# Longer loads and stores, and a release behind the last product, in a bf16 scale-and-add stream

## The chip, the cores and the metric

The kernel runs on one core of a Trainium2 chip. The metric is device time in microseconds (us), as a median of several executions; before and changed kernel were run on the same chip in the same rounds. A trace's *span*, from the first to the last instruction, is about 1.3 us shorter than the time of the execution that was traced. A ratio is the mean time of one kernel's runs over the mean of the other's of the same rounds, so it is not quite the ratio of the medians that are quoted beside it. Two kernels count as different when the ratio is clear of 2%.

## The reference

```python
B, S, D = 1024, 16, 512
x, y: (B, S, D) bf16;  gamma: (D,) bf16
def reference(x, y, gamma):
    return x + gamma * y
```

Flattened, x, y and the result are 16384 x 512. Each of the 128 partitions holds 128 consecutive rows of 512 elements, which is 128 KB. In this text "64 KB" is 64 such rows, the part of one partition; the transfer as a whole has 128 times as much, 8 MB.

## The kernel before

Loads are issued by SyncE, stores by ScalarE, so loads and stores are on two DMA queues (q1 and q10 of the page). VectorE does all the arithmetic: a product in place of y, and then a sum in place of that.

```python
PIECES = [32, 32, 32, 32]
X_AT = [0, 32, 0, 32]           # where in x_sb a piece of x goes: two places, each used twice
X_AFTER = [-1, -1, 0, 1]        # the sum that has to be done before the place is used again
SP = [('x', 0), ('y', 0), ('x', 1), ('y', 1), ('y', 2), ('x', 2), ('y', 3), ('x', 3)]
ACT = [('g',), ('s', 0, 0, 2), ('s', 1, 1, 2), ('s', 2, 2, 2), ('s', 3, 3, 3)]
EARLY = [('x', 0), ('y', 0), ('g',)]       # issued ahead of the start barrier

def _take(sem, n, eng):
    return eng.wait_ge(sem, n).then_inc(sem, -n)
...
    for c in range(n):
        yt = y_sb[:, piece(c), :]
        _take(s_y[c], 16, nc.vector)
        nc.vector.tensor_tensor(
            out=yt, in0=yt, in1=gamma_sb[:, None, :].to_broadcast([P, PIECES[c], D]), op=MULT
        ).then_inc(s_dve, 1)
        _take(s_x[c], 16, nc.vector)
        _take(s_dve, 1, nc.vector)
        nc.vector.tensor_tensor(out=yt, in0=x_tile(c), in1=yt, op=ADD).then_inc(s_add, 1)
```

A store `('s', a, b, k)` writes pieces a to b and waits until sum k is done. The first three stores all wait for sum 2. That is more than their data need: it keeps stores out of the way until the loads are nearly through.

Of the kernel before, what the change touches and what calls it, by code (L numbers as in the profile page):

```python
# [3 lines left out]


PIECES = [32, 32, 32, 32]

X_AT = [0, 32, 0, 32]
X_AFTER = [-1, -1, 0, 1]


SP = [('x', 0), ('y', 0), ('x', 1), ('y', 1), ('y', 2), ('x', 2), ('y', 3), ('x', 3)]
ACT = [('g',), ('s', 0, 0, 2), ('s', 1, 1, 2), ('s', 2, 2, 2), ('s', 3, 3, 3)]

EARLY = [('x', 0), ('y', 0), ('g',)]
MULT, ADD = mybir.AluOpType.mult, mybir.AluOpType.add


def _take(sem, n, eng):


    return eng.wait_ge(sem, n).then_inc(sem, -n)  # L22


def kernel(
    tc: tile.TileContext,
    x: bass.AP,
    y: bass.AP,
    gamma: bass.AP,
    out: bass.AP,  # L30
):



    nc = tc.nc
    P = nc.NUM_PARTITIONS
    tc.close()
    tc.compile()  # L38

    xf = x.flatten_outer_dims()  # L40
    yf = y.flatten_outer_dims()
    of = out.flatten_outer_dims()
    N, D = xf.shape
    rows = N // P
    n = len(PIECES)
    assert sum(PIECES) == rows
    starts = [sum(PIECES[:c]) for c in range(n + 1)]
    dt = xf.dtype
    xv = xf.rearrange("(p n) d -> p n d", p=P)
    yv = yf.rearrange("(p n) d -> p n d", p=P)  # L50
    ov = of.rearrange("(p n) d -> p n d", p=P)

    gamma_row = nc.alloc_sbuf_tensor("gamma_row", [1, D], dt).ap()
    ones_row = nc.alloc_sbuf_tensor("ones_row", [1, P], dt).ap()
    gamma_sb = nc.alloc_sbuf_tensor("gamma_sb", [P, D], dt).ap()
    y_sb = nc.alloc_sbuf_tensor("y_sb", [P, rows, D], dt).ap()
    x_rows = max(a + r for a, r in zip(X_AT, PIECES))
    x_sb = nc.alloc_sbuf_tensor("x_sb", [P, x_rows, D], dt).ap()
    gamma_ps = nc.alloc_psum_tensor("gamma_ps", [P, D], mybir.dt.float32).ap()

    sem = nc.alloc_semaphore
    s_gamma, s_ones, s_ps, s_dve = sem("s_gamma"), sem("s_ones"), sem("s_ps"), sem("s_dve")
    s_x = [sem(f"s_x{c}") for c in range(n)]
    s_y = [sem(f"s_y{c}") for c in range(n)]
    s_add, s_end, s_out = sem("s_add"), sem("s_end"), sem("s_out")

    def piece(a, b=None):
        return slice(starts[a], starts[(a if b is None else b) + 1])

    def x_tile(c):  # L70
        return x_sb[:, X_AT[c] : X_AT[c] + PIECES[c], :]

    early, stores = [], 0

    def ring(eng, what, known=-1):

        nonlocal stores
        for w in what:
            kind, args = w[0], w[1:]
            need = X_AFTER[args[0]] if kind == "x" else args[2] if kind == "s" else -1  # L80
            if need > known:
                eng.wait_ge(s_add, need + 1)
                known = need
            if kind == "g":
                i = eng.dma_start(out=gamma_row, in_=gamma.unsqueeze(0)).then_inc(s_gamma, 16)
            elif kind == "x":
                c = args[0]
                i = eng.dma_start(out=x_tile(c), in_=xv[:, piece(c), :]).then_inc(s_x[c], 16)
            elif kind == "y":
                c = args[0]  # L90
                i = eng.dma_start(out=y_sb[:, piece(c), :], in_=yv[:, piece(c), :])
                i.then_inc(s_y[c], 16)
            else:
                r = piece(args[0], args[1])
                i = eng.dma_start(out=ov[:, r, :], in_=y_sb[:, r, :]).then_inc(s_out, 16)
                stores += 1
            if w in EARLY:
                early.append(i.ins)

    ring(nc.sync, SP)  # L100
    ring(nc.scalar, ACT)


    nc.vector.memset(ones_row, 1.0).then_inc(s_ones, 1)  # L104
    _take(s_ones, 1, nc.tensor)
    _take(s_gamma, 16, nc.tensor)
    nc.tensor.matmul(gamma_ps, ones_row, gamma_row, start=True, stop=True).then_inc(s_ps, 1)  # L107
    _take(s_ps, 1, nc.vector)
    nc.vector.tensor_copy(out=gamma_sb, in_=gamma_ps).then_inc(s_dve, 1)  # L109
    _take(s_dve, 1, nc.vector)  # L110

    for c in range(n):
        yt = y_sb[:, piece(c), :]
        _take(s_y[c], 16, nc.vector)
        nc.vector.tensor_tensor(  # L115
            out=yt, in0=yt, in1=gamma_sb[:, None, :].to_broadcast([P, PIECES[c], D]), op=MULT
        ).then_inc(s_dve, 1)
        _take(s_x[c], 16, nc.vector)
        _take(s_dve, 1, nc.vector)
        nc.vector.tensor_tensor(out=yt, in0=x_tile(c), in1=yt, op=ADD).then_inc(s_add, 1)  # L120


    nc.scalar.sem_inc(s_end, 1)
    _take(s_end, 1, nc.sync)
    _take(s_add, n, nc.sync)
    _take(s_out, 16 * stores, nc.sync)

    main = nc.main_func.blocks[0].instructions
    names = {i.name for i in early}
    for b in nc.main_func.blocks[1:]:  # L130
        for i in [i for i in b.instructions if i.name in names]:
            b.instructions.remove(i)
    for k, i in enumerate(early):
        main.insert(1 + k, i)


# [1 line left out]
_INS = ['x', 'y', 'gamma']  # L138
_OUTS = [((1024, 16, 512), 'bfloat16')]


# [23 lines left out]
```

## Time and profile before

| | before |
|---|---|
| median | 120.41 us (120.14 to 120.46) |
| span of the trace | 119.5 us |
| bytes moved | 50.33 MB, 421 GB/s over the span |
| DMA queues' share of sixteen engines | 66.4% loads, 32.5% stores |
| VectorE busy | 70.2 us, 59% |

How to read it: the DMA share says what bounds the kernel. The page's groups of instructions (operation, result from operands, shape, count, busy us, mean ns, then idle time before them) and its list of DMA issues say what the pieces are:

```profile
L115 DVE TENSOR_TENSOR y_sb<-y_sb,gamma_sb 128x16384 bf16<-128x16384 bf16 x4 | 34.8, 8688 | 18.4 <-DVEq L22 18.4
L120 DVE TENSOR_TENSOR y_sb<-x_sb,y_sb 128x16384 bf16<-128x16384 bf16 x4 | 34.8, 8692 | 0.6
...
x_sb<-in_x_dram SPq DMA_DIRECT2D x4, 4096.0 KB, 21.5
y_sb<-in_y_dram SPq DMA_DIRECT2D x4, 4096.0 KB, 35.4
out_dram<-y_sb ACTq DMA_DIRECT2D x4, 4096.0 KB, 23.8
```

Eight VectorE instructions of 8.69 us each; the only idle time of note, 18.4 us, ends with a wait of its own sequencer (DVEq) for y. Twelve transfers of 4 MB. The prediction below shows the DMA rows, the windows and the timeline.

### The profile page before, as it was taken

The numbers are of one execution on the slowest core, as the hardware profiler recorded it, in microseconds if no ns is written. First come the engines' busy times: TensorE is split into PE (matmuls) and PEld (weight loads), VectorE is DVE, ScalarE is ACT, GpSimd is POOL, SyncE is SP. The second block draws the span as 40 slices with busy tenths as digits, with TensorE's granted clock in tenths as the row PEclk, the third lists the DMA queues.
The fourth block names the chain that finished last, engine by engine and source line by source line (L and its number), as shares of the span: only waits on it lengthen the run. The fifth ranks groups of instructions, "written<-read, shape, count | busy, mean of one in ns | idle before, by whom it ended". The sixth has DMA issues, their size and how long they took to land. (4 is left out here: it accounts for less than half of the span.)

```text
span 119.5 us, 84 instructions
## 1 busy us (share of the span) xinstructions
PE 0.6 (0%) x1; PEld 0.1 (0%) x1; DVE 70.2 (59%) x10; POOL 0.2 (0%) x4
## 2 busy tenths in 40 slices
PE   0100000000000000000000000000000000000000
PEld 0000000000000000000000000000000000000000
DVE  0100000699999289999999999999999600000000
POOL 0000000000000000000000000000000000000000
DMA  7989898998998989898989999898989898989995
GB/s 208 494 373 504 351 526 351 384 493 351 384 493 351 526 351 526 351 515 362 493 384 471 406 428 450 384 493 351 526 351 526 351 526 351 515 362 471 406 471 230
DMA packets 1730, 50.33 MB, mean 421 GB/s; under 512 B 193, under 2 KB 194, under 8 KB 194
## 3 DMA queue, kind: packets, MB, share of 16 engines
q1 hardware_dynamic: 1152, 33.55, 66.4%
q10 hardware_dynamic: 578, 16.78, 32.5%
HBM read 33.56 MB, written 16.78 MB: 421 GB/s over the span
## 5 line engine op out<-in xcount | busy, mean ns | idle before, releaser
L115 DVE TENSOR_TENSOR y_sb<-y_sb,gamma_sb 128x16384 bf16<-128x16384 bf16 x4 | 34.8, 8688 | 18.4 <-DVEq L22 18.4
L120 DVE TENSOR_TENSOR y_sb<-x_sb,y_sb 128x16384 bf16<-128x16384 bf16 x4 | 34.8, 8692 | 0.6
L109 DVE CAST gamma_sb<-gamma_ps 128x512 bf16<-128x512 f32 x1 | 0.7, 692 | 3.4 <-DVEq L22 3.4
L104 DVE MEMSET ones_row<- 1x128 bf16 x1 | 0.2, 165 | 2.0 <-PEq L38 2.0
L107 PE MATMUL gamma_ps<-gamma_row,ones_row 1*128 1x512 bf16 x1 | 0.6, 580 | 4.8 <-PEq L22 4.8
L107 PEld LDWEIGHTS gamma_ps<-gamma_row,ones_row 1*128 1x128 bf16 x1 | 0.1, 100 | 4.8 <-issue 4.8
L149 POOL MEMSET const-bfloat16-1.0<- 128x1 bf16 x1 | 0.1, 101 | 0.0
L149 POOL MEMSET const-uint8-127<- 128x1 uint8 x1 | 0.1, 101 | 0.0
L149 POOL MEMSET const-float32-0.0<- 128x1 f32 x1 | 0.1, 98 | 0.2 <-issue 0.2
L149 POOL MEMSET const-float32-1.0<- 128x1 f32 x1 | 0.1, 98 | 0.0
## 6 DMA issues: line engine op xcount, KB each, us to landing
x_sb<-in_x_dram SPq DMA_DIRECT2D x4, 4096.0 KB, 21.5
y_sb<-in_y_dram SPq DMA_DIRECT2D x4, 4096.0 KB, 35.4
out_dram<-y_sb ACTq DMA_DIRECT2D x4, 4096.0 KB, 23.8
gamma_row<-in_gamma_dram ACTq DMA_DIRECT2D x1, 1.0 KB
```

What stands on the lines that cost most here:

```text
L104: nc.vector.memset(ones_row, 1.0).then_inc(s_ones, 1)
L107: nc.tensor.matmul(gamma_ps, ones_row, gamma_row, start=True, stop=True).then_inc(s_ps, 1)
L109: nc.vector.tensor_copy(out=gamma_sb, in_=gamma_ps).then_inc(s_dve, 1)
L115: nc.vector.tensor_tensor(out=yt, in0=yt, in1=gamma_sb[:, None, :].to_broadcast([P, PIECES[c], D]), op=MULT).then_inc(s_dve, 1)
L120: nc.vector.tensor_tensor(out=yt, in0=x_tile(c), in1=yt, op=ADD).then_inc(s_add, 1)
L149: nc = _bacc.Bacc("TRN2", target_bir_lowering=False, num_devices=1)
```

## The change

The intent is fewer and longer transfers. y and x are loaded in halves of 64 KB rows, both x halves in one place; the stores are of 64, 32 and 32 KB. Since the first store would now be allowed as early as the second sum, before the second x half is even moving, a new semaphore `s_go` is to hold the stores until the last product is over.

```diff
-X_AT = [0, 32, 0, 32]
-X_AFTER = [-1, -1, 0, 1]
 
+SP = [('y', 0, 64), ('x', 0, 64, 0), ('y', 64, 128), ('x', 64, 128, 0)]
+ACT = [('g',), ('s', 0, 64), ('s', 64, 96), ('s', 96, 128)]
...
+DVE = [('m', 0), ('m', 1), ('a', 0), ('a', 1), ('m', 2), ('m', 3), ('go',), ('a', 2), ('a', 3)]
...
+            if kind == "s" and not went and ("go",) in DVE:
+                _take(s_go, 1, eng)
+                went = True
             if need > known:
-                eng.wait_ge(s_add, need + 1)
+                eng.wait_ge(s_add, need)
                 known = need
...
+    for kind, *args in DVE:
+        if kind == "go":
+            nc.vector.sem_inc(s_go, 1)
+            continue
...
+        if kind == "m":
+            need(y_loads, c)
+            g = gamma_sb[:, None, :].to_broadcast([P, PIECES[c], D])
+            nc.vector.tensor_tensor(out=yt, in0=yt, in1=g, op=MULT).then_inc(s_dve, 1)
+            open_mults += 1
```

`('m', c)` is the product of piece c, `('a', c)` its sum. A store now waits, besides `s_go`, only for the sums of its own pieces.

More of the change, by code (lines that the diff above doesn't have):

```diff
@@ L6 @@
 PIECES = [32, 32, 32, 32]
-X_AT = [0, 32, 0, 32]
-X_AFTER = [-1, -1, 0, 1]
-SP = [('x', 0), ('y', 0), ('x', 1), ('y', 1), ('y', 2), ('x', 2), ('y', 3), ('x', 3)]
-ACT = [('g',), ('s', 0, 0, 2), ('s', 1, 1, 2), ('s', 2, 2, 2), ('s', 3, 3, 3)]
-EARLY = [('x', 0), ('y', 0), ('g',)]
+SP = [('y', 0, 64), ('x', 0, 64, 0), ('y', 64, 128), ('x', 64, 128, 0)]
+ACT = [('g',), ('s', 0, 64), ('s', 64, 96), ('s', 96, 128)]
+EARLY = (2, 1)
+DVE = [('m', 0), ('m', 1), ('a', 0), ('a', 1), ('m', 2), ('m', 3), ('go',), ('a', 2), ('a', 3)]
 MULT, ADD = mybir.AluOpType.mult, mybir.AluOpType.add
@@ L56 @@
     y_sb = nc.alloc_sbuf_tensor("y_sb", [P, rows, D], dt).ap()
-    x_rows = max(a + r for a, r in zip(X_AT, PIECES))
+    x_loads = [w for w in SP + ACT if w[0] == "x"]
+    y_loads = [w for w in SP + ACT if w[0] == "y"]
+    stores = [w for w in SP + ACT if w[0] == "s"]
+    for loads in (x_loads, y_loads, stores):
+        assert sum(w[2] - w[1] for w in loads) == rows
+    x_rows = max(w[3] + w[2] - w[1] for w in x_loads)
     x_sb = nc.alloc_sbuf_tensor("x_sb", [P, x_rows, D], dt).ap()
@@ L62, with meets, pieces_of, x_at @@
     s_gamma, s_ones, s_ps, s_dve = sem("s_gamma"), sem("s_ones"), sem("s_ps"), sem("s_dve")
-    s_x = [sem(f"s_x{c}") for c in range(n)]
-    s_y = [sem(f"s_y{c}") for c in range(n)]
-    s_add, s_end, s_out = sem("s_add"), sem("s_end"), sem("s_out")
-    def piece(a, b=None):
-        return slice(starts[a], starts[(a if b is None else b) + 1])
-    def x_tile(c):
-        return x_sb[:, X_AT[c] : X_AT[c] + PIECES[c], :]
-    early, stores = [], 0
-    def ring(eng, what, known=-1):
-        nonlocal stores
-        for w in what:
-            kind, args = w[0], w[1:]
-            need = X_AFTER[args[0]] if kind == "x" else args[2] if kind == "s" else -1
+    s_load = {w: sem("s_" + "_".join(map(str, w[:2]))) for w in x_loads + y_loads}
+    s_add, s_go, s_end, s_out = sem("s_add"), sem("s_go"), sem("s_end"), sem("s_out")
+    added = [a for kind, *a in DVE if kind == "a"]
+    order = {a[0]: k for k, a in enumerate(added)}
+    def meets(a, b, c, d):
+        return a < d and c < b
+    def pieces_of(a, b):
+        return [c for c in range(n) if meets(starts[c], starts[c + 1], a, b)]
+    def x_at(row):
+        return next(w[3] + row - w[1] for w in x_loads if w[1] <= row < w[2])
+    def frees(w):
+        old = x_loads[: x_loads.index(w)]
+        old = [v for v in old if meets(v[3], v[3] + v[2] - v[1], w[3], w[3] + w[2] - w[1])]
+        return [c for v in old for c in pieces_of(v[1], v[2])]
+    early = []
+    def ring(eng, what, n_early):
+        known, went = 0, False
+        for k, w in enumerate(what):
+            kind = w[0]
+            need = frees(w) if kind == "x" else pieces_of(w[1], w[2]) if kind == "s" else []
+            need = max((order[c] + 1 for c in need), default=0)
+            if kind == "s" and not went and ("go",) in DVE:
+                _take(s_go, 1, eng)
+                went = True
             if need > known:
-                eng.wait_ge(s_add, need + 1)
+                eng.wait_ge(s_add, need)
                 known = need
@@ L86, in ring @@
             elif kind == "x":
-                c = args[0]
-                i = eng.dma_start(out=x_tile(c), in_=xv[:, piece(c), :]).then_inc(s_x[c], 16)
+                to = x_sb[:, w[3] : w[3] + w[2] - w[1], :]
+                i = eng.dma_start(out=to, in_=xv[:, w[1] : w[2], :]).then_inc(s_load[w], 16)
             elif kind == "y":
-                c = args[0]
-                i = eng.dma_start(out=y_sb[:, piece(c), :], in_=yv[:, piece(c), :])
-                i.then_inc(s_y[c], 16)
+                r = slice(w[1], w[2])
+                i = eng.dma_start(out=y_sb[:, r, :], in_=yv[:, r, :]).then_inc(s_load[w], 16)
             else:
-                r = piece(args[0], args[1])
+                r = slice(w[1], w[2])
                 i = eng.dma_start(out=ov[:, r, :], in_=y_sb[:, r, :]).then_inc(s_out, 16)
-                stores += 1
-            if w in EARLY:
+            if k < n_early:
                 early.append(i.ins)
-    ring(nc.sync, SP)
-    ring(nc.scalar, ACT)
+    ring(nc.sync, SP, EARLY[0])
+    ring(nc.scalar, ACT, EARLY[1])
     nc.vector.memset(ones_row, 1.0).then_inc(s_ones, 1)
@@ L110, with need @@
     _take(s_dve, 1, nc.vector)
-    for c in range(n):
-        yt = y_sb[:, piece(c), :]
-        _take(s_y[c], 16, nc.vector)
-        nc.vector.tensor_tensor(
-            out=yt, in0=yt, in1=gamma_sb[:, None, :].to_broadcast([P, PIECES[c], D]), op=MULT
-        ).then_inc(s_dve, 1)
-        _take(s_x[c], 16, nc.vector)
-        _take(s_dve, 1, nc.vector)
-        nc.vector.tensor_tensor(out=yt, in0=x_tile(c), in1=yt, op=ADD).then_inc(s_add, 1)
+    landed, open_mults = set(), 0
+    def need(loads, c):
+        for w in loads:
+            if w not in landed and meets(starts[c], starts[c + 1], w[1], w[2]):
+                _take(s_load[w], 16, nc.vector)
+                landed.add(w)
+    for kind, *args in DVE:
+        if kind == "go":
+            nc.vector.sem_inc(s_go, 1)
+            continue
+        c = args[0]
+        yt = y_sb[:, starts[c] : starts[c + 1], :]
+        if kind == "m":
[3 more added lines that the diff above has]
+            open_mults += 1
+        else:
+            need(x_loads, c)
+            if open_mults:
+                _take(s_dve, open_mults, nc.vector)
+                open_mults = 0
+            at = x_at(starts[c])
+            xt = x_sb[:, at : at + PIECES[c], :]
+            nc.vector.tensor_tensor(out=yt, in0=xt, in1=yt, op=ADD).then_inc(s_add, 1)
     nc.scalar.sem_inc(s_end, 1)
@@ L125 @@
     _take(s_add, n, nc.sync)
-    _take(s_out, 16 * stores, nc.sync)
+    _take(s_out, 16 * len(stores), nc.sync)
     main = nc.main_func.blocks[0].instructions
```

## The prediction

Rival A's sum came to 120.6 us: the time before, 120.4, with 0.35 for the restart and 0.1 for the stores added, less a gain from longer transfers. Of that gain only the 0.03 us of five boundaries comes from the trace. B's 120.6 stands on the same parts.

> **What bounds the kernel now.** I read the page's DMA rows first, because the reference is a pure stream: x and y in, x + gamma * y out, 50.33 MB in all.
>
> ```profile
> DMA  7989898998998989898989999898989898989995
> DMA packets 1730, 50.33 MB, mean 421 GB/s; under 512 B 193, under 2 KB 194, under 8 KB 194
> q1 hardware_dynamic: 1152, 33.55, 66.4%
> q10 hardware_dynamic: 578, 16.78, 32.5%
> ```
>
> The row of tenths never falls below 7, and the two queues (q1 the loads, q10 the stores) together fill 98.9% of sixteen engines' span. Next, windows cut where that row seemed to change (columns: busy time of PE, PEld, DVE, POOL, then clock, DMA share, GB/s):
>
> ```profile
> 18.00:39.00 21.00, 0.00 (x0) 0.00 (x0) 16.79 (x2) 0.00 (x0) 1.00 0.98 406
> 39.00:80.00 41.00, 0.00 (x0) 0.00 (x0) 38.14 (x6) 0.00 (x0) 1.00 1.00 432
> 118.00:119.50 1.50, 0.00 (x0) 0.00 (x0) 0.00 (x0) 0.00 (x0) 1.00 0.01 0
> ```
>
> So the kernel is a start, a full pipe, and an end. The trace's packet records say it finer: every large packet is 32 KB, 1536 of them, 96 on each engine; the usual distance between starts on one engine is 1.2094 us; 96 x 1.2094 = 116.1. The rest of the 119.5 us span: first packet 1.0 after the issue, 0.65 longer than later ones, 0.8 lost between 18 and 39 us (packets up to 1.42 us there), 0.35 spread between first and last engine, 0.4 from the last packet to the last landing mark. A DMA boundary costs almost nothing: 1.215 instead of 1.209 us. The timed 120.41 is the span and about 0.9.
>
> VectorE is busy 70.2 us of 119.5 and is not the bound, but it decides when buffers come free and when stores go. The timeline shows that:
>
> ```profile
> 4.83 0.58 PE L107 MATMUL gamma_ps<-gamma_row,ones_row 1*128 1x512 bf16 x1 [4.83 <-PEq L22]
> 22.06 8.69 DVE L115 TENSOR_TENSOR y_sb<-y_sb,gamma_sb 128x16384 bf16<-128x16384 bf16 x1 [15.81 <-DVEq L22]
> ...
> 42.16 8.69 DVE L115 TENSOR_TENSOR y_sb<-y_sb,gamma_sb 128x16384 bf16<-128x16384 bf16 x1 [2.57 <-DVEq L22]
> 51.00 8.69 DVE L120 TENSOR_TENSOR y_sb<-x_sb,y_sb 128x16384 bf16<-128x16384 bf16 x1
> 59.61 8.69 DVE L115 TENSOR_TENSOR y_sb<-y_sb,gamma_sb 128x16384 bf16<-128x16384 bf16 x1
> 59.72 0.33 SPq L88 DMA_DIRECT2D x_sb<-in_x_dram  x1
> ...
> 77.17 17.78 ACTq L95 DMA_DIRECT2D out_dram<-y_sb  x4
> ```
>
> Three things to see. (1) The stores are issued at 77.17, when the last load still has about 3.2 us to run (its last packet ends at 80.42), so the pipe never empties. (2) The product at 59.61 starts before the sum ahead of it is over (51.00 + 8.69 = 59.69), though a wait of VectorE's sequencer stands between them: that sequencer works ahead of the datapath. The trace has it more directly: the wait for x's first piece, behind the product of 22.06, was taken at 22.10, not at 30.75. (3) gamma, on the other queue, had landed by 4.69 and its matmul ran at 4.83, with 16 packets per engine queued on q1 until 21.6: two queues share an engine in turn, they do not wait for each other to empty.
>
> [...]
>
> **The change part by part.** *Fewer, longer transfers.* Twelve DMAs of the large kind become seven, rows of 32 KB become 64 KB except in the last two stores. Five boundaries at 0.006 us are 0.03 us. If rows become packets, an engine has 56 instead of 96[...]. The bytes do not change[...].
>
> *Loads and VectorE.* Landings follow bytes. The first 8 MB land at 21.93 as now, the second (x) at 42.03. Products of pieces 0 and 1 run 22.06 to 39.4, hidden. Sums start at 42.16; two unbroken instructions take 8.61 + 8.69, so they end at 59.46. Only then may the second x half be issued, at about 59.5 (SyncE's issue now follows a sum by 0.03). The second y half drains at 60.7 to 61.06. From a dead start, issue to the effective begin of the stream was 1.0 + 0.65 to 0.85 us, so the stream restarts at about 61.2: a loss of about 0.35 us, instead of none now.
>
> *The release.* VectorE takes y's second half at 61.43 (the sixth 4 MB landed at 61.41), product 2 runs 61.54 to 70.2, product 3 to 78.84. The diff intends the stores to go then. But the release is a semaphore instruction of VectorE's sequencer with nothing to wait for, placed behind the pushed products. The order listing shows it is not attached to a product, and by point (2) the sequencer does not wait for the product's end. With both products pushed at once it fires at about 61.7; ScalarE's other condition, two sums, has been met since 59.5. Then an 8 MB store shares the engines with the 8 MB x load almost from its start. x leads by some 4 us, 61.2 to 65; its other 15.4 us take double, to 95.8, landing at 96.2 instead of 80.8. Sum 2 runs 96.3 to 105.0. Store 0 is through at about 61.2 + 38.7 = 99.9. The second store waits for sum 2: issued at 105.0, flowing at 106.75. So the pipe is dry for about 6.9 us. Sum 3 ends at 113.6, ahead of the second store's end, and the last 8 MB take 19.35: 106.75 + 19.35 + 0.4 = 126.5 span, 127.4 timed. Counting instead in packet turns (x ends at 95.1) gives 126.9. I take 127.0.
>
> **The rivals.** *A, the release works as meant.* It fires at 78.9, stores get their first packet at 79.9 or later against a pipe that drains at 80.4 to 80.8: loss 0 to 0.2. Sums 2 and 3 end at 90 and 98.6, each far ahead of its store's turn. [...] For it: the plain intent of the diff. Against it: the 22.10 mark.
> *B, the sequencer is held until the last product enters the datapath*, 70.15. Store 0 joins at about 73 and x has some 7.5 us left, which take 15: x lands at 88, sum 2 ends at 96.9, store 0 at about 99.9. The second store is issued 3 us ahead of its turn, so the pipe stays full: 120.6 again. For it: before shows only one instruction waiting behind a running one. [...]
> *C, as worked out above*: 127.0, from 125.5 to 129 by how soon the store's packets take turns.
> *D, longer packets or fewer marks are worth more than I find*, or the 0.8 us of slow packets goes away with y first: 119.5 at best. The fixed parts, 116.1 + 1.0 + 0.65 + 0.35 + 0.4 + 0.9 = 119.4, leave no room for 118.0.
>
> **Range and chances.** C gets about 0.62, A and B together 0.36, D's extreme 0.02. A and B lie within 2%. The result is two-peaked, 120 to 121.5 or 125.5 to 129; a range for eight in ten has to reach from 119.8 to 128.8, with 127.0 as the likelier peak.
>
> **What would show it right or wrong.** C is right if ACT's first store is issued at 61 to 63, VectorE idles from 78.8 to about 96 before sum 2, the DMA row has a hole of several us at about 100, and the second store's issue follows sum 2 at about 105. B: first store at about 70.2, no hole. A: first store at 78.9. In all cases the x load should be issued at about 59.5, with a dip of some tenths of a us at 61, and large packets should number 896 if rows are packets. I am wrong in the main if stores issued early do not share with the load (x still landing at 81 with a store issued at 62), or if the release waits for the datapath.

## The result

| | before | changed |
|---|---|---|
| median | 120.39 us (120.14 to 120.46, 6 runs) | 131.41 us (131.19 to 131.95, 6 runs) |
| ratio | | 1.0931, interval 1.0905 to 1.0958 |
| span of the trace | 119.5 us | 130.6 us |
| VectorE busy | 70.2 us | 70.0 us |
| last landing mark of the last x load | 80.84 us | 100.74 us |

It is slower by 11 us. The page of the changed kernel shows where they are (rows of 40 slices of 3.26 us each, busy tenths and GB/s):

```profile
DVE  0020002999993999994999980000000999992000
DMA  9997997997977977979969899989996003899987
GB/s 321 422 542 321 502 462 321 522 442 321 622 341 321 642 321 321 642 321 321 321 301 502 381 402 522 402 361 522 402 422 281 0 0 161 371 432 482 422 381 321
DMA packets 1010, 50.33 MB, mean 385 GB/s; under 512 B 113, under 2 KB 114, under 8 KB 114
q1 hardware_dynamic: 576, 33.55, 61.4%
q10 hardware_dynamic: 434, 16.78, 29.8%
```

The bytes are the same. The DMA row, full to the end before, has a hole of two slices of zero with a 6 and a 3 beside them, and the GB/s row has its two zeros in the same place. VectorE has a gap of some seven slices ahead of its last block of work. The timeline tells what hangs on what:

```profile
41.46 17.29 DVE L154 TENSOR_TENSOR y_sb<-x_sb,y_sb 128x16384 bf16<-128x16384 bf16 x2 [2.14 <-DVEq L21]
58.78 0.33 SPq L106 DMA_DIRECT2D x_sb<-in_x_dram  x1
60.69 17.29 DVE L145 TENSOR_TENSOR y_sb<-y_sb,gamma_sb 128x16384 bf16<-128x16384 bf16 x2 [1.94 <-DVEq L21]
60.88 57.77 ACTq L112 DMA_DIRECT2D out_dram<-y_sb  x3
100.99 17.29 DVE L154 TENSOR_TENSOR y_sb<-x_sb,y_sb 128x16384 bf16<-128x16384 bf16 x2 [23.01 <-DVEq L21]
```

The two products start at 60.69 and end at 77.98. The first store is issued at 60.88, which is 0.2 us after the first of them *started*, 8.4 us before the second one did and 17 us before the end that was meant. (The row of ACTq covers all three stores: the trace has the other two issues at 109.71 and 118.31, each 0.03 us after a sum.) The x load, issued at 58.78, lands only at 100.74, so that VectorE stands still for 23 us before its last two sums. The table of waits gives the same:

```profile
DVE y_sb L154 <- DVEq L21: 25.1, 2, 23.0
DVE y_sb L145 <- DVEq L21: 15.5, 2, 13.5
```

The windows (columns as in the prediction: length, busy times, clock, DMA share, GB/s) show the stages:

```profile
58.00:66.00 8.00, 0.00 (x0) 0.00 (x0) 6.06 (x2) 0.00 (x0) 1.00 0.86 262
66.00:98.00 32.00, 0.00 (x0) 0.00 (x0) 11.98 (x2) 0.00 (x0) 1.00 1.01 436
98.00:102.00 4.00, 0.00 (x0) 0.00 (x0) 1.01 (x1) 0.00 (x0) 1.00 0.42 180
102.00:110.00 8.00, 0.00 (x0) 0.00 (x0) 8.00 (x2) 0.00 (x0) 1.00 0.00 0
110.00:118.00 8.00, 0.00 (x0) 0.00 (x0) 8.00 (x1) 0.00 (x0) 1.00 1.06 455
```

The same cut of the kernel before:

```profile
58.00:66.00 8.00, 0.00 (x0) 0.00 (x0) 8.00 (x2) 0.00 (x0) 1.00 1.06 459
66.00:98.00 32.00, 0.00 (x0) 0.00 (x0) 28.28 (x4) 0.00 (x0) 1.00 0.99 426
102.00:110.00 8.00, 0.00 (x0) 0.00 (x0) 0.00 (x0) 0.00 (x0) 1.00 0.99 426
```

From 66 to 98 the load and the store share the engines and together move as much as ever (436 GB/s). So sharing does not waste the engines there. The loss is after it: nothing at all moves from 102.8 to 110.55, because the first 8 MB of the result are out and the next store waits for sum 2, which waited for x. A smaller loss lies between 58 and 66, where packets of 262 GB/s start, against 459 before; a packet counts where it starts, so the long ones make this look worse than it is.

### The profile page after: what moved, and what is told of

The parts are those of the page before. It is cut to its first block, busy times and chain, and to the rows that moved or that the text cites. A ratio compares the mean times of both kernels' runs of the same rounds, so it can differ in the third digit from the quotient of the medians.

```text
span 130.6 us, 75 instructions
## 1 busy us (share of the span) xinstructions
PE 0.6 (0%) x1; PEld 0.1 (0%) x1; DVE 70.0 (54%) x10; POOL 0.2 (0%) x4
```

## The experiments

My theory (1) after the result: the release runs ahead of the products, load and store then take turns on every engine, x lands 20 us late, and the chain "x, sum 2, second store" leaves the engines dry. Rivals: (2) the long loads into one place are slow by themselves, whatever the release does; (3) mixing loads and stores on the engines costs in itself. Twelve kernels were run; all gave the reference's result. Each is compared with the kernel before in its own rounds. The rounds were on three chips, where the kernel before had medians of 120.31 to 120.66 us, so a few tenths between two rows of the table mean nothing. go_first, no_go, before_early, no_go32 and no_go32b were executed twice, best3 and the changed kernel six times, the others four times. Of rel_end and rel_end32 the interval reaches to both sides of 2%.

Where the text below speaks of packet records, these are the trace's single DMA packets. They do not name their engine; I follow an engine from a packet's end to the packet that starts there. "The slowest engine" is the one whose x data end last.

| run | median us | ratio | interval |
|---|---|---|---|
| changed kernel | 131.41 | 1.0931 | 1.0905 to 1.0958 |
| rel_end | 122.98 | 1.0214 | 1.0175 to 1.0253 |
| rel_mid | 124.56 | 1.0343 | 1.0287 to 1.0398 |
| go_first | 131.20 | 1.0897 | 1.0855 to 1.0939 |
| no_go | 143.25 | 1.1884 | 1.1841 to 1.1926 |
| rows32 | 123.59 | 1.0259 | 1.0226 to 1.0291 |
| before_early | 121.70 | 1.0099 | 1.0048 to 1.0151 |
| before_s64 | 120.44 | 0.9987 | 0.9953 to 1.0021 |
| rel_end32 | 122.81 | 1.0202 | 1.0152 to 1.0252 |
| best1 | 120.90 | 1.0032 | 1.0007 to 1.0057 |
| best3 | 120.69 | 1.0026 | 1.0004 to 1.0048 |
| no_go32 | 125.37 | 1.0412 | 1.0376 to 1.0449 |
| no_go32b | 125.19 | 1.0378 | 1.0310 to 1.0447 |

### rel_end: a release that waits for both products

```diff
-            nc.vector.sem_inc(s_go, 1)
+            nc.vector.wait_ge(s_dve, open_mults).then_inc(s_go, 1)
```

> The release waits for both products' completion marks, so that it comes at their end (about 78 us) and not at 60.75. Theory 1 (the 10 us are the early release alone): the store is issued at 78.1, the x load has the engines to itself and lands at about 81.5, no hole at 103 to 110; 120.9 us, 120.2 to 121.6, with some 0.5 to 1.5 us lost where the x load restarts the pipe at 60. Theory 2 (the long x load in one place is slow by itself): x still lands well after 85 and the time stays over 125.

Measured: 122.98 us. The timeline:

```profile
58.70 0.33 SPq L106 DMA_DIRECT2D x_sb<-in_x_dram  x1
60.62 17.29 DVE L145 TENSOR_TENSOR y_sb<-y_sb,gamma_sb 128x16384 bf16<-128x16384 bf16 x2 [1.94 <-DVEq L21]
78.09 22.32 ACTq L112 DMA_DIRECT2D out_dram<-y_sb  x3
82.74 17.30 DVE L154 TENSOR_TENSOR y_sb<-x_sb,y_sb 128x16384 bf16<-128x16384 bf16 x2 [4.83 <-DVEq L21]
```

Its page has this row in place of the one with the hole:

```profile
DMA  9799779977997799779798799999999889999992
```

The first store now goes at 78.09 and x has landed at 82.5; VectorE's long gap is gone, and so is the hole. One line of the kernel is worth 131.41 - 122.98 = 8.4 of the 11 us. Theory 2 falls as the main cause, but not altogether: the expected 120.2 to 121.6 was missed by 1.4 us. The packet records of this run show two places on the slowest engine. At 60 us, where the x load could only be issued at 58.70 and y's last packet ended at 60.11, the next packet ends 1.4 us later than an unbroken stream would have it. Between 77 and 82 us, where stores follow loads, packets of 2.7 to 3.8 us instead of 2.42 add 1.3. Such terms are not exact to the tenth: rel_end32 below has the same two with 1.7 and 0.8.

### rel_mid and go_first: the place of the release

rel_mid waits for one product's mark:

```diff
-            nc.vector.sem_inc(s_go, 1)
+            nc.vector.wait_ge(s_dve, 1).then_inc(s_go, 1)
```

> The release comes at the end of the first of the two products, 69.4 us. Theory 1: the store shares with the rest of the x load only; x lands at 89 to 92, sum 2 ends at 98 to 101, about when store 0 leaves the pipe dry, so the time is 120.5 to 123.5 us, near the version released at the end. Theory 2: over 125. Were any overlap of a store with the load to cost in proportion to its length, about 126.

Measured: 124.56 us, above my band. The store goes at 69.65 and x lands at 93.1:

```profile
69.65 41.41 ACTq L112 DMA_DIRECT2D out_dram<-y_sb  x3
93.40 17.29 DVE L154 TENSOR_TENSOR y_sb<-x_sb,y_sb 128x16384 bf16<-128x16384 bf16 x2 [15.32 <-DVEq L21]
```

Sum 2 ends at 102.09, and by the packet records an engine then stands for 1.8 us on the mean. So the direction is theory 1's, and x was again later than I had worked out; the reason is under rows32.

go_first keeps the bare release but puts it ahead of both products:

```diff
+            if c == 2:                    # behind the wait for y, in front of product 2
+                nc.vector.sem_inc(s_go, 1)
```

> The changed kernel with the release moved in front of both products, right behind the wait for y's second half. If the release never waited for a product, its place among them does not matter: it fires some 0.1 us sooner and the time is that of the changed kernel, 131.4 us (130.8 to 132.2). If the place behind two products did hold it for part of their time, clearly slower, up to the 143 us of the run without a release.

```profile
60.65 17.29 DVE L146 TENSOR_TENSOR y_sb<-y_sb,gamma_sb 128x16384 bf16<-128x16384 bf16 x2 [2.04 <-DVEq L21]
60.68 57.58 ACTq L112 DMA_DIRECT2D out_dram<-y_sb  x3
100.59 17.29 DVE L155 TENSOR_TENSOR y_sb<-x_sb,y_sb 128x16384 bf16<-128x16384 bf16 x2 [22.65 <-DVEq L21]
```

Measured: 131.20 us, and the same timeline to 0.4 us. In front of the products or behind them, the release is the same: as written it never waited for a product. In the changed kernel's trace the release stands at 60.745, 0.06 us after product 2 began and 8.55 us before product 3 did. So the sequencer had gone past product 3 in the list before that product started, at 69.295.

### no_go: no release at all

```diff
-DVE = [..., ('m', 2), ('m', 3), ('go',), ('a', 2), ('a', 3)]
+DVE = [..., ('m', 2), ('m', 3), ('a', 2), ('a', 3)]
```

> The release is taken out; the first store waits for the two sums alone and goes at 58.8 us, with the x load. If the release as written holds nothing back but 2 us, this is as slow as the changed kernel or a little slower, 131 to 134 us. If it did hold the store for longer in some useful way, clearly more than 135.

```profile
58.73 0.33 SPq L106 DMA_DIRECT2D x_sb<-in_x_dram  x1
58.74 71.09 ACTq L112 DMA_DIRECT2D out_dram<-y_sb  x3
112.17 17.29 DVE L154 TENSOR_TENSOR y_sb<-x_sb,y_sb 128x16384 bf16<-128x16384 bf16 x2 [34.23 <-DVEq L21]
```

Measured: 143.25 us, a miss. The bare release holds the store for only 2 us, and these are worth 12. x lands at 111.9, 11.2 us later than in the changed kernel. Three things differ in the packet records. One x packet per engine goes ahead of the first store packet, where the changed kernel has two; so one store packet more, 2.4 us, lies before x's end. Between 66 and 98 us the packets are longer, 3.01 us for x and 2.68 for the store on the mean, where the changed kernel has 2.42 throughout; seven turns of both make 7 x (3.01 + 2.68 - 4.84) = 6.0 us. And from 66 to 104 us the packets fill only 96.5% of the engines' time (in the changed kernel, from 66 to 98, all of it), which makes some 1.3 us. The sum, 9.7, is about the 9.4 us by which x's data end later on the mean of the engines (105.7 against 96.3). The rest of the 11.2 is that the engines no longer keep together: x's data end between 103.1 and 109.2, in the changed kernel between 95.4 and 98.0. Why packets stretch here and not in the changed kernel I tried to learn with no_go32 and no_go32b, below.

### rows32: shorter store rows, the early release left in

```diff
-ACT = [('g',), ('s', 0, 64), ('s', 64, 96), ('s', 96, 128)]
+ACT = [('g',), ('s', 0, 32), ('s', 32, 64), ('s', 64, 96), ('s', 96, 128)]
```

> The early release stays; the first store of 64 KB rows becomes two of 32 KB rows. If engines take turns by packet, a 64 KB x packet alternates with a 32 KB store packet: x lands at about 90 instead of 100.7, sum 2 ends at about 99, before the first two stores leave the pipe dry at 100 to 103: 121 to 123.5 us. If they share by bytes, or if mixing loads with stores is what costs, nothing changes: 130 to 132 us.

```profile
60.99 49.39 ACTq L112 DMA_DIRECT2D out_dram<-y_sb  x4
92.72 17.29 DVE L154 TENSOR_TENSOR y_sb<-x_sb,y_sb 128x16384 bf16<-128x16384 bf16 x2 [14.63 <-DVEq L21]
```

Measured: 123.59 us, 7.8 less than the changed kernel by nothing but the length of the store's rows. The same bytes of load and store share the engines from the same moment, and x lands at 92.5 instead of 100.7. Sharing by bytes, or a price on mixing (theory 3), would have left it at 131. In the changed kernel's records all sixteen engines take turns by packet: after two packets of x alone, a store and an x packet follow each other six times, 2.42 us each. And here a packet is a row: there are 640 packets of 65536 bytes. A 64 KB x packet (2.42 us) that waits for a 64 KB store packet moves half the time; one that waits for 32 KB (1.21 us) moves two thirds of it.

This run also explains why x was later than I worked out in each case. Compare the last end of an x data packet with the last landing mark of that load (us from the span's start, packet records and landing marks):

| run | rows of the store beside it | last x data | last x mark | between |
|---|---|---|---|---|
| before | none yet | 80.42 | 80.84 | 0.4 |
| rel_end | just starting | 82.15 | 82.50 | 0.35 |
| rows32 | 32 KB | 90.89 | 92.47 | 1.6 |
| no_go32b | 32 KB | 92.30 | 93.88 | 1.6 |
| rel_mid | 64 KB | 90.37 | 93.15 | 2.8 |
| changed | 64 KB | 97.96 | 100.74 | 2.8 |
| no_go | 64 KB | 109.16 | 111.92 | 2.8 |

The mark comes later by one packet of the other queue: 0.35 + 1.21 = 1.56 and 0.35 + 2.42 = 2.77. The packet records show it waiting for a turn: the mark is a packet of 4 bytes of its own on the load's queue. In the changed kernel the last of them starts at 100.374 us, where a store packet ends (100.378), and lands 0.36 us later. In all five runs of the table with stores beside the load it starts so at a store packet's end, and in all seven it lands 0.35 to 0.42 us after its start.

### before_early: the early release in the kernel before

```diff
-ACT = [('g',), ('s', 0, 0, 2), ('s', 1, 1, 2), ('s', 2, 2, 2), ('s', 3, 3, 3)]
+ACT = [('g',), ('s', 0, 0, 1), ('s', 1, 1, 1), ('s', 2, 2, 2), ('s', 3, 3, 3)]
```

> The kernel before with its first two stores released by the second sum, at 59.7 us, as early as the changed kernel's. Theory 1 (what costs is the chain from one long shared load to the sum that releases the next store): here sum 2 is done at 77 and releases the third store, the last x quarter lands at about 101, sum 3 ends at 110 as the other transfers run out: 121 to 122.5 us. If an early release as such cost 10 us: about 130.

```profile
58.81 49.81 ACTq L95 DMA_DIRECT2D out_dram<-y_sb  x4
67.53 8.69 DVE L120 TENSOR_TENSOR y_sb<-x_sb,y_sb 128x16384 bf16<-128x16384 bf16 x1
99.57 8.69 DVE L120 TENSOR_TENSOR y_sb<-x_sb,y_sb 128x16384 bf16<-128x16384 bf16 x1 [11.24 <-DVEq L22]
```

Measured: 121.70 us, as expected. The stores go at 58.8, as early as in the slowest run, and the last sum also starts only at 99.57. But sum 2, at 67.53, has its x from long before and releases the third store at 76.26, so that the engines have work until sum 3 is done. An early release costs 1.3 us where the pieces are short and some sum is always done ahead, and 8.4 where one long load stands between it and the next store. So mixing as such (theory 3) is not what costs the changed kernel its 11 us. That it can cost something, the longer packets of no_go show.

### before_s64, rel_end32, best1, best3: the last two to three us, and whether anything beats the kernel before

before_s64 merges the first two stores of the kernel before into one of 64 KB rows:

```diff
-ACT = [('g',), ('s', 0, 0, 2), ('s', 1, 1, 2), ('s', 2, 2, 2), ('s', 3, 3, 3)]
+ACT = [('g',), ('s', 0, 1, 2), ('s', 2, 2, 2), ('s', 3, 3, 3)]
```

> The kernel before with its first two stores merged into one of 64 KB rows, released at the same moment with 3.2 us of loads still to come. If long store rows cost at the change from loads to stores: 121.3 to 121.8 us. If not, 120.4 (120.1 to 120.7), as before.

Measured: 120.44 us; long store rows cost nothing by themselves. rel_end32 is rel_end with the first store cut in two:

```diff
-ACT = [('g',), ('s', 0, 64), ('s', 64, 96), ('s', 96, 128)]
+ACT = [('g',), ('s', 0, 32), ('s', 32, 64), ('s', 64, 96), ('s', 96, 128)]
```

> Release at the products' end as in the first run of this study, and the first store cut in two of 32 KB rows. That run lost about 1.3 us on its slowest engine where loads change to stores (packets of 2.7 to 3.8 us between 77 and 82 us). If long store rows cause that, it goes and the time is 121.6 us (121.2 to 122.0); if the cause is that the store is issued only some 2 us ahead of the end of the loads, or the long x rows, it stays at 122.9 (122.4 to 123.4).

Measured: 122.81 us, the same as rel_end. So the time does not hang on the length of the store's rows here either, though in the one trace the loss at the change to stores is 0.8 us and the one at 60 us is 1.7. What is left of my list is the long x load or the store's late issue. best1 changes the x loads of rel_end:

```diff
-SP = [('y', 0, 64), ('x', 0, 64, 0), ('y', 64, 128), ('x', 64, 128, 0)]
+SP = [('y', 0, 64), ('x', 0, 32, 0), ('x', 32, 64, 32), ('y', 64, 128), ('x', 64, 96, 0), ('x', 96, 128, 32)]
```

> Release at the products' end, y in 64 KB rows, x in four loads of 32 KB rows with two places, so that the third x load waits for sum 0 alone and is issued at about 50 us, ten before y's end. The restart loss of 1.4 us at 60 us should be gone. If the loss at the change to stores comes from long x rows: 120.2 us (119.8 to 120.6), equal to the kernel before; if from the store's rows or its late issue: 121.5 (121.1 to 121.9).

```profile
48.08 8.93 SPq L106 DMA_DIRECT2D x_sb<-in_x_dram  x2
78.18 17.86 ACTq L112 DMA_DIRECT2D out_dram<-y_sb  x3
78.37 17.29 DVE L154 TENSOR_TENSOR y_sb<-x_sb,y_sb 128x16384 bf16<-128x16384 bf16 x2 [0.37 <-DVEq L21]
```

Measured: 120.90 us, between the two numbers. The third x load is issued at 48.08, far ahead of y's end, and the packet records have no gap and no long packet at 60 us any more. That is what the second place in x's buffer buys. This edit changes the x rows' length too, and rel_end ran on another chip, so the 2.1 us gained over rel_end are not all proven to be that gap. The first store packets still took 3.17 us on the mean instead of 2.42.

best3 releases the store 2 us sooner, at the end of a first part of the last product:

```diff
-PIECES = [32, 32, 32, 32]
+PIECES = [32, 32, 32, 24, 8]
...
-            nc.vector.wait_ge(s_dve, open_mults).then_inc(s_go, 1)
+            nc.vector.wait_ge(s_dve, 2).then_inc(s_go, 1)
```

The list of VectorE's work gets `('m', 4)` ahead of the release and `('a', 4)` at its end.

> The version with x in 32 KB rows and the release at the products' end, with the last product cut in 24 and 8 rows and the release at the end of the 24: at about 76 us instead of 78.1, so that the store is issued about 3 us ahead of the end of the loads, as in the kernel before, and not 1. If the 0.7 us that its first store packets took too long come from the short lead: 120.2 us (119.8 to 120.5), equal to the kernel before. If they come with any first packets of a second queue: 120.9 (120.6 to 121.3).

```profile
76.08 19.90 ACTq L112 DMA_DIRECT2D out_dram<-y_sb  x3
```

Measured: 120.69 us, between the two expectations and not clear of best1 by its time. The packet records say more: all sixteen first store packets take 2.42 us here, against 2.89 to 3.38 in best1, and the last x packet of an engine takes 1.38 to 1.75 us instead of 1.21. So with the longer lead the long first store packets are gone, and a shorter stretch falls on the load in their place. Neither version beats the kernel before; both are within 0.4% of it, on the slow side. With the release mended, long rows bring nothing that can be seen.

### no_go32 and no_go32b: what stretches the packets

no_go with the first store in 32 KB rows:

```diff
-ACT = [('g',), ('s', 0, 64), ('s', 64, 96), ('s', 96, 128)]
+ACT = [('g',), ('s', 0, 32), ('s', 32, 64), ('s', 64, 96), ('s', 96, 128)]
```

> The run without the release (143 us, store and x load issued in the same moment, packets of both stretched to 2.7 to 3.0 us while they share) with the first store in 32 KB rows. By turns of packets x's 8 turns cost 8 x 3.63 = 29 us from 61: landing at 92 to 94, sum 2 done at 102 to 103, about 124 to 125.5 us if packets keep their usual length; if two queues that start in the same moment always stretch each other's packets by a fifth, x lands at 97 or later and the time is 128 us or more.

Measured: 125.37 us, but not a clean test: each short store waits for its own sum only, so the first went at 50.3 us. no_go32b swaps the two, so that both wait for the second sum:

```diff
-ACT = [('g',), ('s', 0, 32), ('s', 32, 64), ('s', 64, 96), ('s', 96, 128)]
+ACT = [('g',), ('s', 32, 64), ('s', 0, 32), ('s', 64, 96), ('s', 96, 128)]
```

> The run before this one let its first 32 KB store go after the first sum, at 50.3 us, which was not intended. Here the two stores change places, so that both wait for the second sum and go at 58.9 us, in the moment of the x load, as in the run without a release. If two queues that start in one moment stretch each other's packets (2.7 to 3.0 us there), they do so here too: x lands at 97 or later, 127.5 us or more. If the stretching needs rows of 64 KB on both queues: packets of 2.42 and 1.21 us, x lands at 91 to 94, 123 to 125 us.

Measured: 125.19 us; both queues start in the same moment (58.69 and 58.70), and x lands at 93.9. By the run's total excess of packet time over the usual lengths, per engine 2.8 us against 8.6 in no_go and 2.9 in the changed kernel, there is no lasting stretch, only some 1.7 us between 60 and 67. So a start in the same moment was not enough here, and sharing was not enough; it took rows of 64 KB on both queues *and* the same moment, in one traced run. What happens there is not settled.

## Why the prediction was right or wrong

**The bound.** Right: 116 us of full engines were there in the changed kernel too, in two parts with a hole between.

**Longer transfers.** Right: 896 large packets, as worked out, and from start to start 2.416 us for 64 KB against 2 x 1.2094 = 2.419 for two of 32 KB. That is 40 x 0.003, some 0.1 us. before_s64 and best1 confirm that nothing is gained.

**Loads and VectorE.** Products and sums ran as worked out, in unbroken pairs of 17.29 us. The x load went at 58.78 instead of 59.5, because the slow packets of 18 to 39 us, 0.8 us of the kernel before's trace, did not come back. They belong to that one execution: before_s64 and before_early have the same loads in the same order, and their traces have no such packets. The restart loss at 60 us was named but mis-sized: 0.35 us said, 1.4 on the slowest engine of rel_end.

**The release.** Right, and shown: by the trace (60.745 against product 2's 60.686), by go_first and by rel_end. One product (it started at 69.295) waited behind a running one while the sequencer went on to the release. Whether more than one can wait was not tried.

**The size: the step that failed.** The time was 131.41 us and lay outside 119.8 to 128.8. The step was "its other 15.4 us take double, to 95.8, landing at 96.2". Measured, x's last data ended at 97.96 and its mark came at 100.74. The doubling itself was right; what it started from, and the mark behind it, were mis-sized. The first 2.2 us are the start of the sharing: on the slowest engine the turns began not at 65 but at 69.0. x's first packet started there at 61.61 and took 2.95 us (2.94 on the mean of the engines), its second, with which the store came in, 4.44 us (3.46 to 4.49); then six store and six x packets took turns, 29.0 us in all. The other 2.4 us are the mark, for which I had 0.4 us as in an unshared queue; it took 2.8. Both terms come before sum 2, and so they are in the end time in full. Later terms are smaller: the second store flowed 0.84 us after its issue and not 1.75 (-0.9), and the last 8 MB with their mark took 20.0 instead of 19.75 (+0.25). 126.5 + 4.5 - 0.9 + 0.25 + 0.2 (sum 2's start after the mark, mostly) = 130.6, the span. From the span to the time I added 0.9 us, the traced span against the median of other executions; within one execution it is 1.3.

**The rivals.** A (a release that works) was put at 120.6; rel_end, which is A built, takes 122.98: I had left out most of the two losses of about 1.4 and 1.3 us. B was put at 120.6, and rel_mid, which releases at nearly the same moment, takes 124.56: x landed at 93.15 and not at 88, with its data 2.4 us late and its mark 2.8 behind them. Had the release worked as meant, the change would still not have paid.

## What to carry to other kernels

An increment that stood alone in VectorE's list was not tied to the instructions in front of it (it came at 60.745 us, their end at 77.98): where it has to mean "this is done", attach it to the instruction or let it wait for the instruction's own mark (the sums' marks and rel_end's wait did so here: stores issued 0.03 us after a sum, and at 78.09). When a store is let in beside a load, ask which later store hangs on that load: here a long load, shared in turns with rows of the same length, landed 42.0 us after its issue, against 23.8 in rel_end, its mark alone waiting for a store packet of 2.42 us, and the engines ran dry behind it for 7.75 us. Short pieces with two places cost nothing here, and made the kernel before nearly indifferent to the same early release (1.3 us).
